# PSUM tiles taken from hand-kept lists, and a new table for the order of all steps, in a chunked RWKV-7 kernel with a low-rank mixer behind it

## The chip, the cores and the metric

The kernel runs on one core of one Trainium2 chip. The metric is device time in microseconds (us) of one execution; the time before is the median of seven.

## What is computed

The reference has two blocks. The first is a recurrence over 768 time steps, for 4 batches of 8 heads with a 40 x 40 state each:

```python
for t in range(S):
    y[:, :, t] = einsum('bhd,bhde->bhe', rt, state)
    Sa = einsum('bhde,bhe->bhd', state, at)
    state_decay = state * wt[:, :, None, :] - einsum('bhd,bhe->bhde', Sa, bt)
    state = state_decay + einsum('bhd,bhe->bhde', vt, kt)
```

Its output, put into the form (4, 768, 320), is `x` of the second block:

```python
h = x.transpose(0, 2, 1) @ U @ V          # low-rank mixing along time, rank 32
u = x + h.transpose(0, 2, 1)
ch = maximum(u @ w_ch1, 0.0) @ w_ch2      # 320 -> 1280 -> 320
return u + ch
```

All is float32.

## The kernel before

**Two phases.** Phase 1 does the recurrence in chunks of 64 time steps. A unit is one chunk of one pair of batches: 2 pairs x 12 chunks = 24 units, numbered 0 to 23, where units 0 to 11 belong to the first pair. Phase 2 is the mixer's two large matmuls (`up_proj`, lines 259 to 265, and `down_proj`, line 273), for six blocks of four chunks.

**The steps of phase 1.** Each unit is worked off by Python generators, and each `next()` of one issues a small step:

- `f` (`prep_f`, 8 steps a unit): clip the decay w (f.1); transpose w and a on TensorE into the PSUM tiles `pw` and `pa`, and scan `pw` on VectorE, line 456 (f.2); multiply `pa` into `fa` (f.3); transpose the scan into `pq`, copied out by ScalarE (f.4); reciprocal on VectorE (f.5); scale b on GpSimd (f.6); transpose it into `pb` (f.7); scores into `pf`, written to DRAM by four DMAs (f.8).
- `l` (`substitute`, 17 steps for a group of units): the triangular inverse, 30 rounds of a multiply and an add, on VectorE for unit 0 (`l0`) and on GpSimd for the groups 1 to 3, 4 to 7, and so on (`l1` to `l6`). A `g` step before it gathers the scores by DMA, and a `t` step after it fetches the result (`td`) for one unit.
- `s` (`prep_s`, 9 steps): transposes of v, r, k (`pv`, `pr`, `pk`), scores (`pe`) and the assembly of the inverse (`pg2`, `px2`).
- `c` (`carry`, 11 steps): the recurrence itself, with the PSUM tiles `ph`, `ps`, `pg`, `pX`, `pn`, `pd`, `pS`.
- `q` and `p` are squares for a range check on ScalarE; capital letters load one input of one unit; `w` loads and narrows the float64 weights of the mixer, seven small steps for each piece; `m` runs the mixer's first block ahead (`hut`, `mix`, `turn`).

Nearly every step that uses TensorE issues one block of matmuls there: 4 of 128 x 128, or 32 small ones. I call that a group. Phase 1 has some 553 of them.

**What sets the order.** A string `ORDER` (line 735) lists 1312 steps, and a loop issues them one by one; a suffix says on which queue a DMA is issued (`s` or none: SyncE, `a`: ScalarE, `x`: half on each). The engines' queues are in order, so the table decides what stands before what on every engine.

**Where PSUM tiles come from.** [...]`one(name)` takes a tile of one bank from a pool of two, `two(name)` one of two banks from a pool of three. Which of the pool's places a tile gets is chosen by the framework when it places the program's tiles:

```python
        def one(name):
            return ps.tile([128, 512], F32, name=name, tag="one", bufs=2)

            pw = one("pw")
            up(wc, pw)
            pa = one("pa")
            up(u.nat["A"], pa)
            nc.vector.tensor_copy(seg[:, :, 0:1], heads(pw[:])[:, :, 0:1])
```

The first matmul into a tile waits for whatever read the place's last tile.

Of the kernel before, what the change touches and what calls it, by code (L numbers as in the profile page):

```python
# [37 lines left out]
def kernel(  # L38
# [138 lines left out]
    def hut(pr, bank, new):  # L177

        ps_ = [bank(f"ph{x}") for x in range(2)]
        for c in range(NCH):  # L180
            for x in range(2):
                nc.tensor.matmul(out=ps_[x][32 * (c % 4):32 * (c % 4) + 32, 0:DM], lhsT=U_[half(x), c, :],
                                 rhs=XTM[half(x), pr * NCH + c, :], start=c < 4, stop=c >= NCH - 4,
                                 skip_group_check=True)
        hs = [new() for _ in range(2)]
        nc.vector.tensor_copy(hs[0][:, 0:DM], ps_[0][:, 0:DM])
        nc.scalar.activation(out=hs[1][:, 0:DM], in_=ps_[1][:, 0:DM], func=ACTF.Copy)
        ts = []
        for x in range(2):
            p = bank("pq")  # L190
            nc.tensor.matmul(out=p[0:RANK, 0:DM], lhsT=IB[:], rhs=hs[x][:, 0:DM], start=True, stop=True)
            ts.append(new()[0:RANK, 0:DM])
            nc.vector.tensor_copy(ts[x], p[0:RANK, 0:DM])
        return ts

    def mix(g, ts, bank):

        pr, th = g // NT, g % NT
        for c in range(th * GC, (th + 1) * GC):
# [5 lines left out]
            nc.vector.tensor_tensor(out=x, in0=p[:, 0:DM], in1=x, op=ALU.add)  # L205
            yield

    def turn(g, bank, new, uf):

        for i in range(3):  # L210
# [10 lines left out]
            if i == 1:  # L221
                nc.scalar.activation(out=t, in_=p[:], func=ACTF.Copy)
            else:
                nc.vector.tensor_copy(t, p[:])
            uf.append(t)
            yield

    def ahead(bank):

        first["ts"] = ts = hut(0, bank, dead)  # L230
        yield
        for g in range(NT):
            for i, _ in enumerate(mix(g, ts, bank)):
# [3 lines left out]
        yield from turn(0, bank, lambda i: dead(), first["uf"])  # L237
# [3 lines left out]
    def part_2(ex, again):  # L241
# [3 lines left out]
        def bank(name):  # L245
            return mps.tile([128, 512], F32, name=name, tag="pm", bufs=2)

# [33 lines left out]
        if again:  # L281
            ts, uf = hut(0, bank, new), []
            for g in range(NT):
                for _ in mix(g, ts, bank):
                    pass
            for _ in turn(0, bank, piece, uf):
                pass
        for g in range(NG):
            hid = mb.tile([128, NJ, 2 * GN], F32, name="hid")
            up_proj(hid, uf, (0, 2))  # L290
            if g + 1 == NT:
                ts = hut(1, bank, new)
            up_proj(hid, uf, (4,))
            if g + 1 < NG and g + 1 >= NT:
                for _ in mix(g + 1, ts, bank):
                    pass
            up_proj(hid, uf, (6, 8))
            if g + 1 < NG:
                uf = []
                for _ in turn(g + 1, bank, piece, uf):  # L300
# [7 lines left out]
    with ExitStack() as p1:  # L308
# [77 lines left out]
        def one(name):  # L386
            return ps.tile([128, 512], F32, name=name, tag="one", bufs=2)

        def two(name):
            return ps.tile([128, 2, 512], F32, name=name, tag="two", bufs=3)  # L390
# [48 lines left out]
        def prep_f(u):  # L439
# [17 lines left out]
                                         initial=1.0, op0=ALU.mult, op1=ALU.add)  # L457
            yield
# [3 lines left out]
            nc.vector.tensor_copy(u.fa[:, :, 0:1], heads(pa[:])[:, :, 0:1])  # L462
            u.fa = u.fa[:].rearrange("p (i x) t -> p i (x t)", x=2)
# [6 lines left out]
            for s, t in enumerate((u.x[:, 0], qo[:])):  # L470
                nc.scalar.activation(out=t, in_=p[:].rearrange("p (i s e) -> p s i e", s=2, e=DP)[:, s, :, 0:D],
                                     func=ACTF.Identity, scale=at0[:, 0:1], bias=at0[:, 1:2])
            across(nc.scalar, u, qo)
# [14 lines left out]
            nc.scalar.activation(out=fb[:].rearrange("p i t -> p (i t)"), in_=p[:], func=ACTF.Copy)  # L488
            yield
# [6 lines left out]
            for q, t in enumerate((fl, u.fh)):  # L496
# [3 lines left out]
                for x in range(2):  # L500
                    nc.sync.dma_start(out=u.fd[x, :, q].rearrange("h (s t) -> s h t", t=LB),
                                      in_=t[64 * x + 32 * q:64 * x + 32 * q + 32])
            yield
# [47 lines left out]
        def prep_s(u):  # L551
# [7 lines left out]
            nc.scalar.activation(out=fv[:].rearrange("p i t -> p (i t)"), in_=pv[:], func=ACTF.Copy)  # L559
            yield  # L560
# [3 lines left out]
            nc.scalar.activation(out=u.fr[:].rearrange("p i t -> p (i t)"), in_=pr[:], func=ACTF.Copy)  # L564
            yield
# [3 lines left out]
            nc.scalar.activation(out=fk[:].rearrange("p i t -> p (i t)"), in_=pk[:], func=ACTF.Copy)  # L569
            yield  # L570
# [16 lines left out]
            masked(u.cm[:], p[:, :, NP * DP:])  # L587
            yield
# [10 lines left out]
            for x in range(2):  # L599
                s = slice(64 * x + 32, 64 * x + 64)  # L600
                nc.scalar.activation(out=GX[s, :, 0:32],
                                     in_=pg[s, 0:NH * 32].rearrange("p (h t) -> p h t", t=32), func=ACTF.Copy)
            yield
            px = one("px2")
            for h in range(NH):
                for x in range(2):
# [4 lines left out]
                                 func=ACTF.Copy)  # L611
            yield
# [3 lines left out]
        def carry(u):  # L616
# [5 lines left out]
            pv = two("ph")  # L622
            for i, s, x in four:
                nc.tensor.matmul(out=pv[half(x ^ s), s, D * i:D * (i + 1)], lhsT=u.e[half(x), s, i, :],  # L624
                                 rhs=vt[half(x), 2 * i + s, 0:D], start=True, stop=True)
            pv = pv[:, :, 0:NP * D].rearrange("p s (i e) -> p s i e", e=D)
# [3 lines left out]
            nc.scalar.activation(out=rs if first else ve[:], in_=pv, func=ACTF.Copy, scale=-1.0)  # L630
            yield
            if not first:
                p = two("ps")
                for i, s, x in four:
# [3 lines left out]
                                        op=ALU.subtract)  # L638
            yield
# [9 lines left out]
            for i in range(NP):  # L649
                for x, s in ((0, 0), (1, 1), (0, 1), (1, 0)):  # L650
# [5 lines left out]
                                 in_=p[:, :, 0:NP * DP].rearrange("p x (i t) -> p x i t", t=DP), func=ACTF.Copy)  # L656
            yield
# [11 lines left out]
            if not last:  # L669
# [3 lines left out]
                nc.scalar.activation(out=nx[:], in_=heads(p[:])[:, :, 0:D], func=ACTF.Copy)  # L673
            yield
# [13 lines left out]
            if not last:  # L688
# [8 lines left out]
                nc.vector.tensor_tensor(out=state["K"][:, :, :, 0:D], in0=dn, in1=pe, op=ALU.mult)  # L697
            yield
# [8 lines left out]
            for s, t in enumerate((u.x[:, 0], yo[:])):  # L707
                nc.vector.scalar_tensor_tensor(out=t, in0=py[:, s], scalar=1.0, in1=u.x[:, s], op0=ALU.mult,
                                               op1=ALU.mult, accum_out=SQ[:, u.n, NCHK - 2 + s:NCHK - 1 + s])
            across(nc.sync, u, yo)  # L710
            yield
            if not last:
# [7 lines left out]
                nc.scalar.activation(out=SV[:], in_=heads(p[:])[:, :, 0:D], func=ACTF.Copy)  # L720
                yield
# [14 lines left out]
W0 W1a B1x A0 V1a f0 A1x B0x p1 f0 W2x q1 f0 A2 f0 K1x f1 q0 f0 f0 R1x f1 f1 w q0 V2 B2x W3x f1 f2 f1 f0 q1 A3x f2  # L736
f3 f0 f1 W4x f2 f2 f2 f1 K0x f3 f3 q3 f4 q2 g0x B3 f1 p2 f2 W5 f3 l0 q3 f3 g1a f2 f3 p1 l0 l0 A4 f2 q4 V0 s1 l0 s0
f3 p1 R0a f4 f3 B4x l0 f5 k g2 p0 f4 B5 f4 g3a l1 W6 l0 q4 l1 A5a f4 s0 q2 s0 s0 f4 A6 q5 l0 s1 f5 s1 l1 l0 p0 f6
R2a w f5 l0 p2 f6 l0 l0 f6 l1 B6 f5 l1 s0 K3 A7x W7x q6 l1 q6 q5 l1 l0 f4 f5 l1 f7 A8x q8 l0 f5 w l1 l0 f6 B7x f4
l0 q7 f5 l1 l1 W9 f7 l0 f6 W8x l0 f7 A9a f6 l1 p0 f5 c0 g4 f7 f7 f6 f7 t0 l1 s0 s0 f6 c0 f7 s0 g5a l1 f7 K2 w c0 w  # L740
l1 s0 f8 g6x f8 c0 l1 l1 g7 s1 f8 c0 c0 c0 t1x l2 f8 q7 A10x l2 l2 c0 s1 c0 s1 c0 B8 s1 f8 l2 s1 c0 c1 s1 f8 c1 s2
W10 q10 f10 c1 f9 l2 p2 V3x c1 s2 f8 w c1 c1 s2 q8 q9 t2 f9 c1 f9 c1 l2 c1 R3 V4 s2 f8 c1 t3 f9 s2 l2 s2 s3 l2 s3
f9 s2 s2 w c2 p3 l2 c2 l2 R4x c1 B9 p3 s2 w c2 p3 s3 A11x f10 f10 p4 c2 W12x s3 K4 W11x c2 w B10 f9 l2 c2 c2 f10
s3 c2 c2 c2 A12 f9 q9 V5 R5 s3 s3 w q10 f11 l2 c2 c3 p4 c3 s3 w s4 s4 l2 f9 l2 l2 s3 c3 q12 s4 s4 B11x l2 l2 f10
c3 K5 p5 R6x f11 t4x W13 f11 w c3 c3 s4 t5 s4 f10 B12x c3 f10 c3 q11 f11 c3 c3 s5 c4 A13 f11 p5 s4 s4 c3 f10 f12
c4 p5 s4 f11 s5 c4 f11 w s5 w g8 f13 V6 c4 f11 s5 g10 c4 s5 c4 f12 s5 p6 c4 s5 w q12 g11 p4 f12 g9a K6x l3 f12 c4
t6 c4 c5 w l3 s5 c4 c5 V7x c4 q13 s6 s6 s5 f12 f13 A14 p6 q11 c5 f13 W15 p6 c5 w f12 A15x s6 w s6 c5 w K7x W14 l3
s6 R7 l3 f14 c5 l3 s6 c5 t7 c5 l3 l3 q14 p7 R8 B13 s6 f13 s6 c5 f13 c5 c6 c5 c6 q15 l3 w s6 p7 f13 f14 V8 f14 q13
c6 l3 p7 f15 c6 s7 w B14 c6 w c6 l3 f12 f14 f12 f14 s7 c6 s7 c6 f13 s7 w s7 l3 c6 f15 W16 f15 w l3 l3 q14 K9 V9a
l3 R9x s7 w A17 f13 s7 w K8 s7 f15 c6 l3 c7 c6 w W17x c7 l3 s7 s8 s8 g12x c7 c7 l3 f15 c7 A16a c7 g13x s8 c7 c7  # L750
B15 p8 f14 t8 s8 f14 f15 s8 p9 s8 f14 c7 p9 f15 c7 f16 s8 s8 f15 w g14 c7 c8 q15 s8 q17 s9 g15x B16 W18 p8 c8 l4
c8 s9 s9 V10 c8 f16 R10 f17 t9 l4 p8 c8 q16 K10 l4 c8 c8 f16 w c8 s9 A18 W19x f16 s9 c8 s9 s9 l4 R11 c8 p9 c8 K11
s10 s10 l4 l4 f16 s9 c9 t10 V11 f16 s10 p10 s9 w w l4 l4 c9 f17 c9 f17 c9 s10 s10 B17 A19 q16 w c9 f17 f17 c9 p11
f17 l4 l4 p11 s10 f19 f16 c9 c9 c9 s10 V12 p11 c9 B18 p10 s11 s10 s11 l4 c10 l4 l4 q19 c9 s11 c10 l4 s10 t11 R12
c10 R13 W21 f18 p10 f17 K12 f18 q18 c10 f18 f16 c10 A20 q17 s11 c10 l4 w s11 f19 W20x p12 K13x q18 l4 c10 f19 s11
p12 f18 s11 c10 c10 l4 c10 B19 s11 f18 t12 f20 c10 f19 c11 c11 g16a s11 c11 s12 s12 s12 c11 V13 s12 f19 f18 f17 w
s12 s12 V14x s12 f21 A21x f18 c11 s12 c12 f18 s12 w c12 f20 c11 c12 c11 c11 p12 K14a t13 f19 c11 c12 f19 c11 q20
s13 f20 c12 f19 s13 s13 w g18 s13 R14 p13 c12 c12 g19a s13 W22a s13 f21 c12 g17x c12 l5 f21 w w l5 s13 V15 c12 q21
B20 q19 s13 p14 w w f20 c12 w c13 l5 s14 s13 c13 p13 B21 l5 f20 f20 A23 p14 R15 s14 s14 c13 c13 t14 p13 f21 A22 l5
c13 K15 w W23 l5 l5 s14 c13 t15x c13 p15 w f22 s14 s14 q20 c13 f20 s14 c14 c13 f21 w q21 c14 l5 s14 c13 p15 c13  # L760
# [164 lines left out]
```

## Time and profile before

| what | value |
|---|---|
| median of 7 runs | 839.5 us (835.47 to 852.36) |
| the profiled execution | 846.28 us, its span 844.5 us |
| granted TensorE clock, mean | 0.889 |
| busy: TensorE matmul / VectorE / GpSimd / ScalarE | 708.4 / 412.3 / 298.7 / 254.2 us |

In the names of the profile, PE is TensorE's matmuls, PEld its weight loads, DVE VectorE, ACT ScalarE, POOL GpSimd, SP SyncE; a q behind a name is that engine's DMA queue. Busy time says nothing of what waits for what; for that there are the waits (who sat idle until what ended), the timeline (instructions in order of time) and the windows (busy time in stretches of the span). Phase 2 begins at about 541 us.

### The profile page before, as it was taken

The page shows a single profiled execution, that of the slowest core. Times are in us where ns is not written, and L with a number is a line of the kernel's source. Part 1 is how long each engine was busy: PE and PEld are TensorE (multiplying, and loading weights), DVE is VectorE, ACT ScalarE, POOL GpSimd, SP SyncE. Part 2 cuts the span into 40 slices and gives each one's busy share as a digit, 9 for nine tenths or more (in the row PEclk, how much of TensorE's full clock was granted, in tenths as well). Part 3 has the DMA queues.
Part 4 walks back from the last instruction along what each step waited for, and adds up shares of the span by engine and source line. Part 5 has one row for each costly group of instructions (what it writes and reads, how often), then busy time and mean ns, then how long its engine had stood idle before and what let it go on. Part 6 is the DMA issues. An engine that isn't in the chain of part 4 may idle for free.

```text
span 844.5 us, 30102 instructions
## 1 busy us (share of the span) xinstructions
PE 708.4 (84%) x13146; PEld 505.0 (60%) x13146; DVE 412.3 (49%) x854; ACT 254.2 (30%) x662; POOL 298.7 (35%) x541
## 2 busy tenths in 40 slices
PE   4543778798788878887886888899999999999996
PEld 2433667687676767776774776446473553735554
DVE  7899657577836664796675677210112112121110
ACT  2432345454553643554343444010101001000000
POOL 3457478227717640782698445000000000000000
PEclk9755599888987896799797899799999999999998
DMA  7553445655545464646453432001010010100101
GB/s 126 100 106 54 86 76 94 113 93 85 88 105 89 82 120 72 111 77 132 86 105 101 98 91 62 5 1 32 0 24 9 4 28 0 24 9 8 24 8 26
DMA packets 241386, 53.87 MB, mean 64 GB/s; under 512 B 233728, under 2 KB 236832, under 8 KB 241248
## 3 DMA queue, kind: packets, MB, share of 16 engines
q1 hardware_dynamic: 182864, 42.14, 25.9%
q10 hardware_dynamic: 58384, 9.74, 6.8%
q8 instruction: 105, 1.72, 0.9%
q14 instruction: 33, 0.27, 0.1%
HBM read 37.68 MB, written 10.22 MB: 57 GB/s over the span
## 4 chain that ended last, share of the span: by engine, by line
PE 65%; DVE 10%; DMA 7%; issue 7%; POOL 4%; ACT 3%; SPq 2%; ACTq 1%; DVEq 0%; POOLq 0%
PE p L273 15%; PE p L259 13%; PE p L262 4%; PE px L608 3%; PE pS L717 3%; PE pe L430 2%; PE pg L597 2%; PE pd L681 1%; PE ph L624 1%; PE pg L704 1%; PE pq L424 1%; PE ps L635 1%; PE pX L652 1%; PE pv L202 1%; PE pg L663 1%
## 5 line engine op out<-in xcount | busy, mean ns | idle before, releaser
L273 PE MATMUL p<-ip,hid 128*128 128x320 f32 x384 | 107.3, 432 | 0.0
L531 POOL TENSOR_TENSOR ln<-ln,tmp 128x30 f32<-128x30 f32 (+19 forms) x180 | 97.9, 544 | 14.1
L529 POOL TENSOR_TENSOR tmp<-ln 128x30 f32<-128x30 f32 (+19 forms) x180 | 93.8, 521 | 12.1
L259 PE MATMUL p<-uf,W 128*128 128x512 f32 x200 | 95.4, 621 | 0.0
L264 ACT ACTIVATE hid<-p 128x512 f32<-128x512 f32 x30 | 17.9, 597 | 256.9 <-PE p L262 256.9
L273 PEld LDWEIGHTS p<-ip,hid 128*128 128x128 f32 x384 | 73.0, 190 | 30.4
L265 DVE TENSOR_SCALAR hid<-p 128x512 f32<-128x512 f32 x30 | 20.7, 692 | 127.0 <-PE p L262 127.0
L259 PEld LDWEIGHTS p<-uf,W 128*128 128x128 f32 x200 | 37.5, 195 | 53.0 <-issue 52.2
L276 DVE TENSOR_TENSOR o<-p,XTM 128x320 f32<-128x320 f32 x24 | 11.8, 492 | 117.3 <-PE p L273 117.3
L478 DVE RECIPROCAL ip<-ip 128x320 f32<-128x320 f32 x24 | 51.7, 2153 | 0.8
L554 POOL TENSOR_TENSOR nKT<-nK,ip 128x320 f32<-128x320 f32 x24 | 21.9, 914 | 56.4 <-PE pg L704 32.6
L483 POOL TENSOR_TENSOR nBT<-nB,ip 128x320 f32<-128x320 f32 x24 | 20.7, 864 | 58.1 <-DMA nB<-in_b_dram 18.6
L717 PE MATMUL pS<-ID,SK 64*64 64x64 f32 x704 | 30.0, 238 | 7.9 <-issue 6.0
L608 PE MATMUL px<-t,GX 32*64 32x32 f32 x768 | 32.3, 235 | 2.6 <-issue 2.1
L717 PEld LDWEIGHTS pS<-ID,SK 64*64 64x64 f32 x704 | 26.4, 150 | 9.5 <-issue 6.8
L608 PEld LDWEIGHTS px<-t,GX 32*64 32x64 f32 x768 | 29.2, 152 | 4.8 <-issue 2.7
L419 PE MATMUL pw<-ID,nWC 128*128 128x128 f32 x96 | 21.7, 367 | 11.0 <-DVE nWC L444 10.8
L424 PE MATMUL pq<-ID,PF 128*128 128x128 f32 x96 | 19.9, 343 | 13.1 <-DVE PF L456 10.0
L456 DVE TENSOR_TENSOR_SCAN PF<-pw,seg 128x512 f32<-128x512 f32 x24 | 29.4, 1225 | 2.6 <-DVE pw L455 0.5
L419 PE MATMUL pa<-ID,nA 128*128 128x128 f32 x96 | 20.5, 353 | 11.8 <-issue 9.6
L273 PE MATMUL p<-fa,hid 128*128 128x320 f32 x96 | 30.4, 439 | 0.0
L262 PE MATMUL p<-uf,W 64*128 64x512 f32 x100 | 28.2, 641 | 0.0
(171 smaller groups left out, 1415.0 us busy)
## 6 DMA issues: line engine op xcount, KB each, us to landing
raw<-in_moe_w_ch_dram SPq DMA_DIRECT2D x18, 320.0 KB, 3.3
out_dram<-o SPq DMA_DIRECT2D x48, 80.0 KB, 2.0
nB<-in_b_dram SPq DMA_DIRECT2D x39, 80.0 KB, 3.4
nV<-in_v_dram SPq DMA_DIRECT2D x38, 80.0 KB, 2.8
nK<-in_k_dram SPq DMA_DIRECT2D x36, 80.0 KB, 3.8
nW<-in_w_dram SPq DMA_DIRECT2D x34, 80.0 KB, 3.2
nA<-in_a_dram SPq DMA_DIRECT2D x34, 80.0 KB, 3.0
td<-ln SPq DMA_DIRECT2D x5, 512.0 KB, 3.0
```

Of the source, the lines that this page charges most:

```text
L259: nc.tensor.matmul(out=ps_[x][:], lhsT=W1[i][:, (j + x) * 128:(j + x + 1) * 128], rhs=uf[i], start=(i == 0), stop=False)
L262: nc.tensor.matmul(out=ps_[x][:], lhsT=W1[2][half(x), (j + x) * 128:(j + x + 1) * 128], rhs=uf[2][half(x)], start=False, stop=True)
L273: nc.tensor.matmul(out=p[:, 0:DM], lhsT=hid[:, f, 2 * j * L:2 * (j + 1) * L], rhs=W2[f], start=(f == 0), stop=(f == NJ - 1))
L419: nc.tensor.transpose(out=p[:, 128 * i:128 * (i + 1)], in_=t[:, 2 * i:2 * i + 2, :].rearrange("p h e -> p (h e)"), identity=ID[:])
L424: nc.tensor.transpose(out=p[:, 128 * i:128 * (i + 1)], in_=t(i), identity=ID[:])
L456: nc.vector.tensor_tensor_scan(out=pf[:, 1:], data0=pw[:], data1=seg[:].rearrange("p h t -> p (h t)"), initial=1.0, op0=ALU.mult, op1=ALU.add)
L478: nc.vector.reciprocal(out=u.ip[:], in_=u.ip[:])
L529: eng.tensor_tensor(out=x, in0=ln[:, 0:j, j:j + 1].to_broadcast([m, j, n]), in1=ln[:, j:j + 1, j + 1:].to_broadcast([m, j, n]), op=ALU.mult)
L531: eng.tensor_tensor(out=ln[:, 0:j, j + 1:], in0=ln[:, 0:j, j + 1:], in1=x, op=ALU.add)
L554: nc.gpsimd.tensor_tensor(out=kt[:, :, 0:D], in0=u.nat["K"][:], in1=u.ip[:], op=ALU.mult)
L608: nc.tensor.matmul(out=px[half(x), 32 * h:32 * h + 32], lhsT=GX[s, h, :], rhs=u.t2[s, h, :], start=True, stop=True)
L717: nc.tensor.matmul(out=p[half(s), 64 * (2 * i + x):64 * (2 * i + x + 1)], lhsT=state["K"][half(s), i, x, :], rhs=ID[half(s), half(s)], sta ...
```

## The change

The pools `one` and `two` become objects that hold their tiles for the whole of phase 1 and hand out the one that was given back first, in the order in which the Python code issues its steps. A call of `back` is put behind the last reader of each tile, also in the mixer's steps that run ahead; phase 2 keeps its own pool and passes a `back` that does nothing. The steps, their instructions and their number stay the same.

```diff
-        def one(name):
-            return ps.tile([128, 512], F32, name=name, tag="one", bufs=2)
-
-        def two(name):
-            return ps.tile([128, 2, 512], F32, name=name, tag="two", bufs=3)
+        class Banks:
+            def __init__(self, name, n, shape):
+                self.free = [ps.tile(shape, F32, name=f"{name}{i}") for i in range(n)]
+            def __call__(self, name):
+                return self.free.pop(0)
+            def back(self, *tiles):
+                self.free.extend(tiles)
+        one = Banks("one", 2, [128, 512])
+        two = Banks("two", 3, [128, 2, 512])
...
             nc.vector.tensor_tensor_scan(out=pf[:, 1:], data0=pw[:], data1=seg[:].rearrange("p h t -> p (h t)"),
                                          initial=1.0, op0=ALU.mult, op1=ALU.add)
+            one.back(pw)
             yield
...
             nc.vector.tensor_copy(u.fa[:, :, 0:1], heads(pa[:])[:, :, 0:1])
+            one.back(pa)
```

The table `ORDER` is new from its first line to its last; it has the same 1312 steps, and other queues for some of the loads. The stretch before the first step of the recurrence (`c0`), and the one around the first `m`:

```diff
-l0 q7 f5 l1 l1 W9 f7 l0 f6 W8x l0 f7 A9a f6 l1 p0 f5 c0 g4 f7 f7 f6 f7 t0 l1 s0 s0 f6 c0 f7 s0 g5a l1 f7 K2 w c0 w
...
+f3 g2a l0 g3x q4 p1 f5 k R0 l0 q2 V2a W6x l0 l1 q4 q5 s0 f4 s0 f4 f5 f6 p0 l1 R2x s0 l1 l0 l1 A6 q3 A7 f5 l0 f4 s0
+f4 f5 q7 l1 B5 f6 p1 f5 l0 l1 w q6 W7 l1 q5 p2 l1 p2 f6 l1 f4 s1 l0 f7 B7 A8x l0 l0 s1 l0 l0 l0 B6x c0 f5 l0 q7 W9
+W8x f5 g4x f6 f7 t0 f6 w p0 K2a l1 f6 l1 f7 f7 f6 f6 s1 f7 f8 f7 c0 c0 l1 s0 s0 f7 l1 s0 f7 g5a s0 p1 c0 w q6 l1
...
-w w s19 c18 s19 w l6 w R21a p19 K21a w w l6 w l6 l6 c19 c19 w w m w s20 w p21 w p20 w w c19 s20 c19 t20 s20 c19
...
+s19 w c18 w t19 w l6 w c18 s19 c18 V21a l6 w l6 p18 R21a R20a p18 s19 w K20a w V20a w p21 s19 w w w p20 l6 w p19 m
```

## The prediction

> **What bounds the kernel now.** I read the page first, then the windows, then the waits, then the timeline at the two longest TensorE waits that no data explains.
>
> The page's busy rows and 40 slices of 21.1 us each:
>
> ```profile
> PE 708.4 (84%) x13146; PEld 505.0 (60%) x13146; DVE 412.3 (49%) x854; ACT 254.2 (30%) x662; POOL 298.7 (35%) x541
> ...
> PE   4543778798788878887886888899999999999996
> ...
> DVE  7899657577836664796675677210112112121110
> ...
> PEclk9755599888987896799797899799999999999998
> ```
>
> Three stages can be seen. In slices 1 to 5 VectorE is full and TensorE half idle at a half clock; in slices 6 to 25 TensorE is at seven to eight tenths; from slice 26 (541 us) it is at nine: phase 2, some 303 us, which the change does not touch. So 541 us can move.
>
> The windows say how each stage is limited (columns: stretch, length, then busy us of PE, PEld, DVE, ACT, POOL with counts, granted clock, DMA share, GB/s):
>
> ```profile
> 80.00:90.00 10.00, 3.40 (x71) 3.02 (x72) 9.36 (x18) 0.89 (x4) 5.65 (x10) 0.50 0.36 63
> 90.00:100.00 10.00, 6.88 (x139) 5.89 (x137) 5.89 (x11) 4.67 (x12) 7.27 (x17) 0.67 0.46 86
> 100.00:110.00 10.00, 9.67 (x220) 8.09 (x220) 3.73 (x8) 2.88 (x6) 2.88 (x8) 0.59 0.51 116
> ...
> 300.00:350.00 50.00, 41.43 (x1137) 36.44 (x1140) 26.43 (x60) 20.71 (x54) 14.89 (x34) 0.73 0.54 98
> 350.00:400.00 50.00, 39.64 (x1432) 33.95 (x1427) 41.17 (x80) 25.80 (x67) 32.58 (x57) 0.99 0.53 102
> ```
>
> At 80 to 90 us VectorE is full; at 90 to 110 it does 9.6 of 20 us while TensorE catches up. From about 100 us TensorE is the bound: its gaps between 100 and 541 us add up to 37 us, those before 100 us to 43 (the timeline's gaps over 0.3 us).
>
> The waits of TensorE and VectorE in phase 1 (total, times, longest):
>
> ```profile
> DVE tt L574 <- DMA nT<-td: 24.7, 7, 5.3
> ...
> PE pw L419 <- DVE nWC L444: 10.8, 4, 7.6
> ...
> PE pa L419 <- issue: 9.6, 2, 7.8
> ...
> PE pb L419 <- POOL nBT L483: 6.7, 4, 4.0
> ...
> PE pq L191 <- DVE fa L186: 6.2, 1, 6.2
> ...
> PE pg L597 <- DVE tt L574: 5.4, 3, 2.7
> ```
>
> The third row is odd: `pa` needs only a loaded input. The timeline at the longer of its two waits, then at the other, and a group at full clock for size:
>
> ```profile
> 77.78 1.06 PE L419 MATMUL pw<-ID,nWC 128*128 128x128 f32 x4
> ...
> 85.28 1.23 DVE L456 TENSOR_TENSOR_SCAN PF<-pw,seg 128x512 f32<-128x512 f32 x1
> ...
> 86.61 1.09 PE L419 MATMUL pa<-ID,nA 128*128 128x128 f32 x4 [7.76 <-issue]
> ...
> 323.53 1.22 DVE L456 TENSOR_TENSOR_SCAN PF<-pw,seg 128x512 f32<-128x512 f32 x1
> ...
> 324.86 1.09 PE L419 MATMUL pa<-ID,nA 128*128 128x128 f32 x4 [1.85 <-issue]
> ...
> 330.97 0.66 PE L419 MATMUL pv<-ID,nV 128*128 128x128 f32 x4
> ```
>
> Both times `pa` starts 0.1 us after the scan of its own unit's `pw` ends. In the compiled program of the kernel before, which shows each tile's bank and each semaphore wait, these two `pa` (units 7 and 16) lie in the bank of their own `pw`, so TensorE stands until VectorE has scanned it. The code issues `pa` before the scan; the pool still chose that place, though another tile's reader had been issued earlier.
>
> **The change, part by part.**
>
> *Placement.* Comparing that program's banks with the rule "first given back in the order of issue" on the old table, 24 of 444 tiles have another predecessor: the two `pa`, the tiles that swap with them, three other swaps in the one-bank pool, and seven swaps of `pg` with `pX`. The swaps are worth nothing: `pX` waits 0.8 us in all. The first matmul into a pool tile also waits for TensorE itself (154 times in that program), which a kept tile would not need; these semaphore instructions take 0.05 us ahead in the weight queue, so 0 to 2 us, taken as 0. What counts is 7.76 + 1.85 = 9.6 us of TensorE standing still. The 1.85 at 323 us lies where TensorE is the bound: -1.9. The 7.76 is bounded by 0 (VectorE was 94% busy meanwhile) and 7.76; VectorE's 10.4 us of idle in the 20 us after it says that TensorE's lag came back, so I take all: -7.8.
>
> *The start of the new table.* Its own PSUM waits: unit 5's `pa` is taken at f5.2 and held to f5.3, and between them `pv`, `pq` and `pr` follow each other in the one bank left, each behind the last one's reader: a scan (0.07 + 0.17 + 1.23), a copy (0.60), two half copies (0.97), 3.0 us together. Unit 7's `pq` follows `pa` directly and waits for its scan, 1.5 us. So +4.5, and the start gives -3.3 net. As a check I summed work by mean durations up to c1's first step: 66 TensorE groups and 96 us of VectorE in the old table, 67 and 94 in the new. No more than 2 to 4 us is in that.
>
> *DMA waits in the steady stage.* In TensorE groups (480 from c1 at 113.9 us to c23 at 520.3 us: 0.85 us each) I counted how far a transfer's issue lies ahead of its use. Writing `td` took 5.7 us in the chain of waits and fetching it 3.4, together 11 groups. From the last `l` step to the first unit's `tt` the old table leaves 4, 6, 5, 7, 13.6, 9, 13 groups, 24 short; the new 8, 5.6, 15, 11, 7, 14.6, 12, which is 12 short, but three later fetches are only 1 to 2 groups ahead, 8 more. 20 for 24, of the 10.0 us that `pg` of line 597 waits (5.4 and 4.6 more put down to issue): -1.5. Loads of w: twice 0 groups and once 1 in the old table, none under 2 beyond unit 3 in the new; of 10.8 us 7.6 is the first unit's and stays: -2 of the other 3.2. Loads of b get longer leads (shortest 2, 3, 4 against 2, 6, 9): -2 of 6.7. Loads of k get shorter ones (2, 3, 6 against 5, 5.6, 6): +1.5, GpSimd being late for `pk`.
>
> *Queues.* DMAs issued on ScalarE go from 99 to 90 (each about 0.65 us), on SyncE from 309 to 318. ScalarE is half busy: 0. SyncE's transfers move later by 6 us spread over 540: 0, and at most +2 where one queues behind a blocked write.
>
> *The mixer's start.* The 6.2 us of `pq` of line 191: VectorE stood behind GpSimd, which had three `l6` steps ahead of the narrowing it waited for. In the new table TensorE is there 8.6 groups (7.3 us) earlier and GpSimd has three `l6` steps and a weight piece (8 us by their rows) less to do: -1, bounds -6 and +3.
>
> *Nearer neighbours.* `pq` directly behind its scan's `pw`, 4 times for 2; one is counted above: +1.5. `pf` directly behind `pb`, 3 for 2: +0.8.
>
> Sum: -1.9 - 3.3 - 1.5 - 2 - 2 + 1.5 - 1 + 2.3 = -7.9.
>
> *The clock.* The 50-us windows from 100 to 541 give about 116 us at the half clock, where a group takes 1.09 us for 0.66: 116 x 0.39 = 45 us lost, more than the 37 us of gaps. The Trainium skill ("TensorE: Matmul & The Clock Gate", "What's actually happening") says that the clock halves after at least one idle window of about 3.4 us. By that rule only the 6.2-us gap at 450 us costs clock here, and shorter waits saved bring nothing: -7.9. The rows disagree: at 300 to 350 us the clock is 0.73 and no gap there exceeds 2.2 us. In proportion (45 us for 37 us of gaps) the 5 us of gaps saved after 100 us would bring 6 more: -14. I take one shortened stretch of about 5 us, 5 x 0.39 = -2, and keep 0 and -6 for the range.
>
> -9.9 in all, on the profiled execution's 846.3: 836.4. That execution is 6.8 us above the median of the runs shown; as the waits that go are set by order, not by that excess, I take them whole from the median: 829.6, rounded to 830.
>
> **The rivals.** About 0.5%, 4.2 us, is what a measurement of this kernel can tell from no change.
>
> *The start is VectorE's.* Then neither the 7.8 nor the 4.5 counts, -7.9 + 3.3 - 2 and no clock leave about -5 to -3: 836. For it: 94% busy at 80 to 90 us. Against: the idle VectorE after it. Same side of nothing: 837, within the bound.
>
> *The one-bank chain at f5.2 (slower).* The chain's first wait is a scan, and the scan for the `pw` of 77.78 us, done at 78.8, began 6.4 us later, behind VectorE's other work. If it does so at f5.2 and again at unit 7's `pq`, 2 x 6 us more come in: TensorE stands as before, in two places, and `c0` with it. With +12 the sum is +2, and with the k loads and the mixer's start at their bad ends (+4 and more) 846. It decides from about 6 us of delay at each scan: below 4 us each the sum stays under zero. For it: only two banks, and VectorE full. Against: in the new table just two `l0` steps are issued between f5.2 and f5.3, and they stand behind the scan, not before it.
>
> *TensorE stays warm.* All of the proportional clock gain, and the mixer's start at its good end: -14 - 5 = -19, 821.
>
> *The placement does nothing* (the pool's choice comes back by other waits) is part of the first rival.
>
> **How the numbers follow.** Forecast (830, between 820 and 835): 0.48. Warm TensorE (821, down to 814): 0.16. VectorE's start (837): 0.20. One-bank chain (846): 0.16. Faster by over 0.5%: 0.48 + 0.16 = 0.64; within: 0.20; slower: 0.16. The range leaves out a few per cent below 815 and the upper half of the slower case: 815 to 846.
>
> **What would show it.** Right: no wait of `pa` on "issue" in the waits; `c0` near 82 us and `c1` near 111; TensorE's gaps from 100 us to the start of phase 2 at about 32 us for 37; waits of `tt` on `td` near 20 us; phase 2 starting near 531 and still 303 us long. Wrong: `pv` of unit 0 or `pq` of unit 7 waiting over 5 us for a scan; `nKT` waits on its load above 30 us; a granted clock in 100 to 541 us below before's 0.87; or phase 2 not of the same length.

## The result, and the profile after

| | before | after |
|---|---|---|
| median | 840.49 us (829.66 to 859.35, 63 runs) | 831.35 us (821.51 to 839.47, 26 runs) |
| the profiled execution, its span | 846.28, 844.5 us | 832.25, 830.5 us |
| granted TensorE clock, mean | 0.889 | 0.896 |

The ratio is 0.991, with a 95% interval of 0.9885 to 0.9934: faster by 0.9%; the medians lie 9 us apart. A second measurement of the same kernel among the experiments gave 0.9944 (0.99 to 0.9988). The forecast was 830. The time came out as forecast; most of the sum behind it did not.

In the changed kernel all one-bank tiles are called `one` and all two-bank tiles `two`. Old lines 419, 424, 430, 456, 191, 574 and 597 are now 435, 440, 446, 472, 192, 598 and 622. The page's rows, 40 slices of 20.8 us each:

```profile
PE 703.9 (85%) x13146; PEld 500.5 (60%) x13146; DVE 400.2 (48%) x854; ACT 253.2 (30%) x662; POOL 296.3 (36%) x541
...
PE   3645799789888789887848899899999999999996
...
DVE  6888677567657747575645757111102112021110
...
PEclk9856599989999969799877978999999999999998
```

The same three stages. Phase 2 now begins at 523.6 us (before: 537.0, and not 541, as the prediction has it) and lasts 306.9 us (before 307.5). So 13.4 us of this pair of executions are gained ahead of it. The profiled execution of before is one of its slower ones, 5.8 us above the median, and that of after is 0.9 above, so some 5 of the 13.4 us are no part of the change. The windows that answer to those of before, in the same columns:

```profile
80.00:90.00 10.00, 2.21 (x8) 1.44 (x8) 9.41 (x23) 1.38 (x5) 3.70 (x8) 0.50 0.50 91
90.00:100.00 10.00, 8.86 (x171) 7.61 (x172) 4.43 (x8) 4.87 (x13) 8.48 (x19) 0.50 0.38 65
100.00:110.00 10.00, 9.53 (x335) 8.06 (x337) 6.60 (x18) 3.99 (x13) 6.57 (x16) 0.91 0.55 120
```

At 80 to 90 us TensorE works even less than before (2.21 us for 3.40) while VectorE is as full (9.41 for 9.36). The timeline there shows what took the place of the wait of `pa`:

```profile
78.10 1.11 PE L435 MATMUL one<-ID,nA 128*128 128x128 f32 x4
...
83.68 1.23 DVE L472 TENSOR_TENSOR_SCAN PF<-one,seg 128x512 f32<-128x512 f32 x1
...
84.96 1.12 PE L440 MATMUL one<-ID,PF 128*128 128x128 f32 x4 [5.75 <-DVE PF L472]
```

`pa` of unit 7 now starts directly behind its `pw`, and then TensorE stands 5.75 us at `pq`, the next tile, for the same scan. The scan comes late because VectorE is behind: it is busy for 9.41 of the 10 us. Whether it matters which TensorE step waits for it, `hand_seq` below tells.

The waits of the changed kernel that answer to those shown of before (total, times, longest):

```profile
DVE tt L598 <- DMA nT<-td: 19.4, 10, 6.4
...
PE one L440 <- DVE PF L472: 12.7, 7, 5.7
...
PE one L192 <- DVE fa L186: 8.5, 1, 8.5
...
PE one L435 <- DVE nWC L460: 8.4, 2, 7.6
...
PE one L435 <- POOL nBT L502: 5.9, 2, 3.3
...
PE one L192 <- ACT fa L187: 5.2, 1, 5.2
...
PE one L622 <- DVE tt L598: 4.9, 3, 2.5
```

The long wait of `pa` on issue is gone. The mixer's start, line 192, has two waits, 13.7 us together, for 6.2. One window from 100 us to the start of phase 2, of before and then of after, shows both parts of the gain:

```profile
100.00:536.90 436.90, 362.90 (x11528) 309.89 (x11524) 283.08 (x611) 198.43 (x528) 245.49 (x418) 0.87 0.49 93
```

```profile
100.00:523.60 423.60, 354.88 (x11485) 302.85 (x11483) 274.61 (x612) 196.06 (x528) 243.36 (x417) 0.88 0.50 96
```

Of 13.3 us, TensorE's idle time gives 5.3 (74.0 to 68.7) and its busy time 8.0: nearly the same matmuls, run faster. This is one pair of executions; the experiments ask what makes the matmuls run faster.

### The profile page after: what moved, and what is told of

Read it like the earlier page. It is cut to its first block, busy times and chain, and to the rows that moved or that the text cites. A ratio compares the mean times of both kernels' runs of the same rounds, so it can differ in the third digit from the quotient of the medians.

```text
span 830.5 us, 30105 instructions
## 1 busy us (share of the span) xinstructions
PE 703.9 (85%) x13146; PEld 500.5 (60%) x13146; DVE 400.2 (48%) x854; ACT 253.2 (30%) x662; POOL 296.3 (36%) x541
## 4 chain that ended last, share of the span: by engine, by line
PE 58%; POOL 9%; DMA 9%; DVE 8%; issue 7%; SPq 5%; ACT 3%; ACTq 1%; POOLq 0%; DVEq 0%
PE p L280 16%; PE p L266 14%; PE one L435 4%; PE p L269 4%; POOL tmp L550 3%; POOL ln L552 3%; PE two L446 2%; PE one L634 2%; PE two L712 2%; PE one L750 2%; DMA fd<-fh 2%; SPq L521 2%; PE one L440 2%; SPq L340 2%; DMA nR<-in_r_dram 1%
## 5 line engine op out<-in xcount | busy, mean ns | idle before, releaser
L550 POOL TENSOR_TENSOR tmp<-ln 128x30 f32<-128x30 f32 (+19 forms) x180 | 93.9, 521 | 12.3
L283 DVE TENSOR_TENSOR o<-p,XTM 128x320 f32<-128x320 f32 x24 | 11.8, 492 | 117.3 <-PE p L280 117.3
L634 PE MATMUL one<-t,GX 32*64 32x32 f32 x768 | 30.8, 232 | 2.3 <-issue 1.2
L440 PE MATMUL one<-ID,PF 128*128 128x128 f32 x96 | 19.7, 340 | 14.9 <-DVE PF L472 12.6
L750 PE MATMUL one<-ID,SK 64*64 64x64 f32 x704 | 31.0, 249 | 0.8 <-issue 0.8
L634 PEld LDWEIGHTS one<-t,GX 32*64 32x64 f32 x768 | 27.9, 148 | 4.9 <-issue 1.9
L472 DVE TENSOR_TENSOR_SCAN PF<-one,seg 128x512 f32<-128x512 f32 x24 | 29.4, 1225 | 2.3
L750 PEld LDWEIGHTS one<-ID,SK 64*64 64x64 f32 x704 | 27.9, 161 | 2.0 <-issue 1.0
L435 PE MATMUL one<-ID,nR 128*128 128x128 f32 x96 | 19.2, 332 | 11.5 <-DMA nR<-in_r_dram 5.6
L544 POOL TENSOR_SCALAR_AFFINE_SELECT ln<-ln 128x1024 f32<-128x1024 f32 (+2 forms) x7 | 8.8, 1264 | 55.8 <-DMA ln<-fd 42.6
L435 PE MATMUL one<-ID,nWC 128*128 128x128 f32 x96 | 20.4, 350 | 9.5 <-DVE nWC L460 8.4
```

The lines of the kernel that those rows point to most:

```text
L435: nc.tensor.transpose(out=p[:, 128 * i:128 * (i + 1)], in_=t[:, 2 * i:2 * i + 2, :].rearrange("p h e -> p (h e)"), identity=ID[:])
L440: nc.tensor.transpose(out=p[:, 128 * i:128 * (i + 1)], in_=t(i), identity=ID[:])
L472: nc.vector.tensor_tensor_scan(out=pf[:, 1:], data0=pw[:], data1=seg[:].rearrange("p h t -> p (h t)"), initial=1.0, op0=ALU.mult, op1=ALU.add)
L550: eng.tensor_tensor(out=x, in0=ln[:, 0:j, j:j + 1].to_broadcast([m, j, n]), in1=ln[:, j:j + 1, j + 1:].to_broadcast([m, j, n]), op=ALU.mult)
L634: nc.tensor.matmul(out=px[half(x), 32 * h:32 * h + 32], lhsT=GX[s, h, :], rhs=u.t2[s, h, :], start=True, stop=True)
L750: nc.tensor.matmul(out=p[half(s), 64 * (2 * i + x):64 * (2 * i + x + 1)], lhsT=state["K"][half(s), i, x, :], rhs=ID[half(s), half(s)], sta ...
```

## The experiments

Ratios are to the kernel before, in runs on the same chip; those of one paragraph can be compared directly unless it says otherwise.

**The two halves alone.** `hand_old` is the changed kernel with the old table, `pool_new` the old kernel with the new table.

```diff
 # hand_old: the changed kernel
-ORDER = """ (new table)
+ORDER = """ (old table)
 # pool_new: the kernel before
-ORDER = """ (old table)
+ORDER = """ (new table)
```

> The kept tiles with the OLD table: the placement alone. Theory A (the gain is mostly the two waits of pa behind its own scan, 9.6 us of TensorE): 831 to 834 us against 840, no wait of pa on a scan, c1 some 5 to 8 us earlier than at 113.9 us. Theory B (the gain is the table; the long wait of 7.76 us lay beside a full VectorE and costs nothing): 837 to 840 us, only the 1.85-us wait in the steady stage is saved.

> The pools with the NEW table: the table alone. In its program one pa (unit 7) still lies in the bank of its own pw. Theory A: the table alone brings little, 836 to 840 us, with a long wait of pa on its scan at about 80 us. Theory B: nearly all of the gain, 830 to 833 us, though that wait is there.

`hand_old`: 837.65 us, ratio 0.9879 (0.9815 to 0.9943). `pool_new`: 849.48 us, 1.0053 (1.0019 to 1.0087). The kept tiles bring the whole gain, and the table by itself loses 4.5 us. With kept tiles the table changes nothing that can be seen (0.9879 without it, 0.991 and 0.9944 with it, in other sets of runs). My working gave the table a gain of its own.

**The stall at the mixer's start.** `m_early` puts the first `m` of the changed table 25 steps earlier (what was expected says 27, a miscount). Run with the two above:

```diff
-... s19 w c18 w t19 w l6 w c18 s19 c18 V21a ... l6 w p19 m
+... s19 w c18 w t19 w l6 w c18 m s19 c18 V21a ... l6 w p19
```

> The changed kernel with the first m step (hut) moved 27 steps ahead, in front of step s19.5 (the transpose of tt, which waits for a DMA). In the changed kernel TensorE stands 8.5 and 5.2 us in hut, because its two copies are queued on VectorE behind tt and a narrowing that waits for GpSimd, and on ScalarE behind loads. Theory A (the waits are in the queues ahead of the copies, and TensorE is the bound there): both waits under 2 us in all and 820 to 825 us against 831. Theory B (GpSimd, behind with the last substitution, sets the pace of this stage whatever TensorE does): the waits go elsewhere, 829 to 832 us.

It gave 833.17 us, ratio 0.9779 (0.9703 to 0.9855; six runs). The waits of its TensorE from 400 to 450 us:

```profile
PE one L634 <- ACT GX L626: 8.9, 1, 8.9
...
PE one L192 <- DVE fa L186: 0.7, 1, 0.7
```

The stall has moved from line 192 to `px2`, line 634. The ratio is lower than the changed kernel's in another set of runs, but a change of place alone does not show why; see `early_16`.

**Which pool.** `hand_two` keeps the two-bank tiles and lets the framework's pool place the one-bank tiles; `hand_one` is the reverse. `after_again` is the changed kernel.

```diff
 # hand_two
-one = Banks("one", 2, [128, 512])
+one = Pooled("one", 2, [128, 512])      # ps.tile(..., tag="one", bufs=2); back() does nothing
 # hand_one
-two = Banks("two", 3, [128, 2, 512])
+two = Pooled("two", 3, [128, 2, 512])
```

> The changed kernel itself, on the same chip as the three below, so that they can be set against it. Every theory: 0.991 of the kernel before, within half a per cent.

> New table; the two-bank tiles kept by hand, the one-bank tiles from their pool as before (one pa again in the bank of its pw; some 150 first matmuls wait for TensorE's own semaphore). Theory A (what the pools cost lies in the one-bank pool): like the new table with both pools, 1.003 to 1.007 of before. Theory C (it lies in the swaps of pg, ps and pX among the two-bank tiles, 14 here): 0.990 to 0.994.

> New table; the one-bank tiles kept by hand, the two-bank tiles from their pool. Theory A: 0.990 to 0.994 of before, as the changed kernel. Theory C: 1.003 to 1.007.

`after_again` 836.25 us, 0.9944 (0.99 to 0.9988). `hand_two` 848.27, 1.0026 (0.9993 to 1.0059). `hand_one` 839.98, 0.9935 (0.9891 to 0.9979). So the gain lies in the one-bank tiles: 0.8%, 7 us, with intervals that do not meet. The two-bank tiles matter nothing that can be seen.

`hand_two` has the wait of `pa` of unit 7 back (8.1 us on issue in its waits), yet the first copy of `c1` comes at 110 us in it, at 111 in the profile after and at 112 in that of `after_again`. The wait that I had put first among the gains does not move the start.

**The weights' narrowing.** In the same set of runs, `narrow16` gives VectorE six weight pieces that GpSimd narrowed, to shorten what stands ahead of the mixer's start:

```diff
-            todo = dst, raw, nc.vector if n < 10 else nc.gpsimd
+            todo = dst, raw, nc.vector if n < 16 else nc.gpsimd
```

> The changed kernel with six more pieces of the mixer's weights narrowed wholly on VectorE instead of half on GpSimd (three operations a piece: 2.6 us of GpSimd become 2.0 us of VectorE). Theory A (the 8.5 and 5.2 us of TensorE in hut hang on GpSimd, which is full from 400 to 450 us and gives the weight buffers back late): both shrink by half or more and the time is 3 to 8 us below the changed kernel. Theory B (GpSimd's last substitution sets the pace, or VectorE's added 12 us come back as waits): within 2 us of it, or slower by up to 5.

833.18 us, ratio 0.984 (0.9761 to 0.9918), which overlaps `after_again`'s interval: a gain of 1% is possible and not shown. The first stall remained (the narrowing now stands on VectorE ahead of the mixer's copy); of its waits from 400 to 450 us:

```profile
PE one L192 <- DVE fa L186: 8.9, 1, 8.9
PE two L712 <- issue: 1.3, 1, 1.3
PE one L192 <- ACT fa L187: 1.2, 1, 1.2
```

**Where the tiles lie, or how they are given out.** A kept tile and a pool tile differ in two things: the bank, and the release. A new pool tile makes its first matmul wait for everything that used the place's last tile, TensorE's own matmuls among it. In the compiled programs TensorE waits for its own semaphore 30 times in the changed kernel and 176 times in `hand_two` (the traces show 12 and 158, the same difference); all engines issue the same work in the same order in both. Only four pairs of one-bank tiles of `hand_two` have changed places with each other; the last is `pa` of unit 7 with the tile behind it. Two kernels separate the two things. `hand_seq` has kept tiles in the pool's banks; `pool_seq` has pool tiles, one pool of a single buffer per bank, in the changed kernel's banks.

```diff
 # hand_seq
-                return self.free.pop(0)
+                return self.free.pop(self.calls in (14, 18, 29))     # for the one-bank tiles
...
-            pa = one("pa")
-            up(u.nat["A"], pa)
+            pa = one("pa") if u.n != 7 else pw       # unit 7: pa is issued behind the scan
 # pool_seq
-                return self.free.pop(0)
+                k = self.free.pop(0)
+                t = ps.tile(self.shape, F32, name=name, tag=f"{self.name}{k}", bufs=1)
```

> The changed kernel's persistent tiles, but its one-bank tiles in the banks that the pool chose: one choice reversed at the pb of unit 2, at the pw of unit 5 and at the pr of unit 1, and the pa of unit 7 in its own pw's bank, issued after the scan. Every engine does the same work in the same order as in hand_two; only the releases differ. Theory A (where the tiles lie, above all the own bank of unit 7): about 848 us, ratio 1.002 like hand_two, c1 at 111. Theory B (a pool tile makes TensorE wait on its own semaphore, some 146 more waits than persistent tiles): about 836, ratio 0.994 like the changed kernel, although the pa of unit 7 waits some 8 us at 76 us.

> The mirror image: the one-bank tiles lie where the changed kernel has them, but each bank is a pool of one buffer, so every tile is a new pool tile that waits for the last release, and TensorE has 148 waits on its own semaphore more than in the changed kernel. No pa waits on issue. Theory A (where the tiles lie): about 836 us, ratio 0.994. Theory B (the pool's extra waits on TensorE): about 848, ratio 1.002, and a mean granted clock near 0.88 against 0.90.

`hand_seq` 830.25 us, 0.9888 (0.9828 to 0.9948); `pool_seq` 842.5 us, 0.9993 (0.9961 to 1.0025). It is the release and not the place. In `hand_seq` the wait I had counted as 7.76 us is there in full, 8.43 us, and the kernel is as fast as the changed one; its timeline:

```profile
76.15 1.06 PE L436 MATMUL one<-ID,nWC 128*128 128x128 f32 x4
85.64 1.12 PE L436 MATMUL one<-ID,nA 128*128 128x128 f32 x4 [8.43 <-DVE PF L474]
```

**Both small changes together.** In the same set, `early_16` is `m_early` and `narrow16` in one kernel.

> The changed kernel with the first m moved in front of the first c18-s19 steps (as m_early) and the weight pieces 10 to 15 narrowed on VectorE (as narrow16). If the two small gains are independent: narrow16 1.0 % and m_early up to 1 % below the changed kernel, ratio 0.975. If both only take away the same stall, which comes back at px2 or at the mixer's copies: ratio 0.984 to 0.99, no better than narrow16 alone.

828.94 us, ratio 0.985 (0.9781 to 0.9919), no better than `narrow16` alone and not to be told from `hand_seq` beside it. The wait at line 192 is 0.9 us, and another has come up at `pS`, line 750:

```profile
PE one L750 <- DVE SK L728: 6.4, 1, 6.4
```

So the mixer's stall is worth little: something else stands there when it goes. This kernel has the lowest median of all, but it is not shown to beat the changed one.

**Which of the waits.** The last two kernels split `pool_seq`: a bank's tile is made anew only for some names, and otherwise used on.

```diff
 # pool_seq, then:
+                t = self.now.get(k)
+                if t is None or name in ("pv", "pq", "pn", "pr", "pg2", "ph0", "ph1", "pu"):   # fresh_on
+                if t is None or name in ("pb", "pS", "pk", "pa", "pw", "px2"):                 # fresh_apart
                     t = ps.tile(self.shape, F32, name=name, tag=f"{self.name}{k}", bufs=1)
```

> As pool_seq (the changed kernel's banks, one pool of one buffer per bank), but a bank's tile is made anew only for pq, pv, pr, pg2, pn and the mixer's tiles ahead; for the others the bank's present tile is used on, as in the changed kernel. TensorE has 113 waits on its own semaphore (changed kernel 30, pool_seq 178): 93 ride on a matmul, 20 stand in an instruction of their own; its separate semaphore instructions are 240 (192, 269). Theory N (every own wait costs the same): 83 of pool_seq's 148 more waits, 56 % of a loss of 0.7 %: ratio 0.997. Theory E (only own waits that stand in an instruction of their own cost, because they hold up the loads ahead): 15 of 63 of them: ratio 0.994 to 0.995, like the changed kernel. Theory I (every added instruction costs): 48 of 77: ratio 0.9975.

> The other half of fresh_on: a bank's tile is made anew only for pw, pa, pb, pk, px2 and pS. TensorE has 98 waits on its own semaphore, 45 on a matmul and 53 in an instruction of their own; its separate semaphore instructions are 224. Theory N (every own wait): 68 of 148, ratio 0.996. Theory E (own waits in an instruction of their own): 48 of 63, ratio 0.998. Theory I (every added instruction): 32 of 77, ratio 0.996. If neither half shows a loss, the two halves need each other or pool_seq's loss is smaller than its interval says.

`fresh_on` 844.95 us, 0.9987 (0.9957 to 1.0016); `fresh_apart` 838.68 us, 0.989 (0.9858 to 0.9923). `fresh_on` lies near theories N and I; `fresh_apart` fits none of the three. As far as the intervals tell, the first set carries the whole loss and the second none, although it has three quarters of the additional waits that stand in an instruction of their own (48 of 63). So neither these instructions nor the number of own waits by itself is the cost: `hand_one` has 115 of them, 85 more than the changed kernel, at no loss either. What matters is at which tiles the release changes: `pq`, `pv`, `pr`, `pg2`, `pn` and the mixer's tiles.

**Where the time goes.** Two windows of each kernel, from the first copy of `c19` to that of `c21`, and from there to phase 2; the work in them is the same. `hand_seq` and `fresh_apart`, which keep the gain:

```profile
442.90:475.80 32.90, 28.32 (x1052) 24.65 (x1050) 22.31 (x57) 15.64 (x40) 15.34 (x18) 0.95 0.47 105
475.80:524.20 48.40, 41.02 (x1213) 31.99 (x1205) 32.58 (x84) 18.42 (x47) 20.82 (x25) 0.89 0.27 65
```

```profile
455.50:485.80 30.30, 27.73 (x1044) 24.47 (x1043) 24.06 (x58) 15.46 (x40) 16.39 (x20) 0.95 0.55 122
485.80:531.30 45.50, 39.63 (x1218) 31.53 (x1211) 30.70 (x82) 18.75 (x47) 19.99 (x24) 0.92 0.27 64
```

`pool_seq` and `fresh_on`, which lose it:

```profile
444.30:479.40 35.10, 32.93 (x1055) 28.45 (x1052) 22.75 (x58) 15.60 (x40) 15.29 (x19) 0.78 0.44 100
479.40:534.60 55.20, 48.36 (x1211) 37.84 (x1203) 32.59 (x83) 18.66 (x47) 20.76 (x25) 0.72 0.23 57
```

```profile
449.50:484.20 34.70, 32.33 (x1041) 28.54 (x1036) 22.87 (x58) 15.63 (x39) 15.69 (x19) 0.80 0.48 107
484.20:539.80 55.60, 49.78 (x1219) 38.94 (x1212) 30.87 (x83) 18.63 (x47) 20.09 (x25) 0.71 0.22 52
```

The stretch takes 81.3 and 75.8 us in the first two, 90.3 and 90.3 in the other two. TensorE's idle time does not explain it (12.0 and 8.4 us for 9.0 and 8.2); its busy time does (69.3 and 67.4 for 81.3 and 82.1), at a clock of 0.89 to 0.95 for 0.71 to 0.80. Most other kernels with the new table fall on the same sides: 81.8 us in the profile after and 82.1 in `after_again` (clock 0.80 to 0.93 in both), 89.7 in `hand_two` and 85.4 in `pool_new`. `hand_one`, which keeps the gain, lies between with 86.0, in an execution 4.7 us above its median.

These are single executions, and this stretch is not always the place. `hand_two` is 10 us later than `after_again` at `c19` already, and `fresh_apart` 6 us later there than `fresh_on`. In the kernel before, whose table has other steps around it, the stretch takes 82.9 us although its tiles come from pools; of the 13.4 us against the profile after, 12.3 lie between 100 us and `c19`, 11.8 of them busy time.

The timeline shows one place. In `hand_seq`, then in `pool_seq`, the same three groups:

```profile
486.32 0.63 PE L657 MATMUL two<-nV,e 64*64 64x40 f32 x32
486.88 0.66 PE L441 MATMUL one<-ID,xf 128*128 128x128 f32 x4
...
488.90 0.69 PE L628 MATMUL one<-tt,fh 32*32 32x32 f32 x32
```

```profile
484.97 0.50 PE L461 MATMUL two<-fr,fv 64*64 64x64 f32 x18 [1.41 <-issue]
...
488.97 1.04 PE L666 MATMUL two<-nV,e 64*64 64x40 f32 x32
489.94 1.11 PE L455 MATMUL pn<-ID,xf 128*128 128x128 f32 x4
...
492.86 1.06 PE L637 MATMUL pg<-tt,fh 32*32 32x32 f32 x32
```

No group waits there in either; each takes 1.04 to 1.11 us for 0.63 to 0.69. In the 8 us ahead of them `pool_seq` has one wait of 1.41 us and one of 0.34, `hand_seq` one of 0.80, and one of 1.42 just ahead of that.

The record of the clock says what stands between. It changes in steps of 3.4 us. Two such stretches of `pool_seq`, then of `hand_seq`:

```profile
483.70:487.10 3.40, 2.13 (x89) 1.80 (x90) 1.61 (x3) 1.26 (x5) 1.73 (x3) 1.00 0.29 90
487.10:511.00 23.90, 23.90 (x454) 18.09 (x450) 12.11 (x30) 6.07 (x14) 7.65 (x9) 0.50 0.24 56
```

```profile
480.60:497.60 17.00, 15.05 (x508) 11.59 (x508) 11.04 (x25) 7.12 (x19) 8.09 (x10) 1.00 0.30 69
497.60:504.50 6.90, 6.90 (x114) 5.31 (x112) 3.15 (x8) 2.16 (x4) 2.37 (x4) 0.51 0.18 50
```

In `pool_seq` the step from 483.7 us, which holds the 1.41-us wait, has 2.13 us of matmuls; the clock then halves and stays at half for 23.9 us, in all of which TensorE is busy. What keeps it there is in the traces too: how much of the array the matmuls of a step use. Give each matmul a weight, the rows of the array that it uses times the columns that it uses times the columns of data streamed through, with 1 for 128 x 128 x 128. Then a group of four transposes weighs 4, and the 32 small matmuls of `px2` together weigh 1. The seven half-clock steps of `pool_seq` weigh 9.7, 7.6, 5.1, 6.7, 4.5, 9.3 and 14.0, and after the last the clock is full. In the 14 traces, from 100 to 530 us, each of the 966 steps that weigh over 12 is followed by a step at full clock, and of the 241 that weigh under 7 only 11 are. One limit at 9.5 tells the next step's clock in 91% of all 1762 steps; the best limit on busy time does so in 83%. This is a pattern found in the traces afterwards: no kernel here was written to try it.

Over all runs of a set the mean granted clock points the same way: 0.9021 and 0.8823 in `after_again` and `hand_two`, 0.8987 and 0.887 in `hand_seq` and `pool_seq`, 0.8899 and 0.8853 in `fresh_apart` and `fresh_on`. In 840 us, 0.02 of clock is 34 us at the half clock, and at 0.39 us lost per us there (a group takes 1.09 us for 0.66) 13 us. By this estimate the three pairs come to 13, 8 and 3 us. That is not the whole account: `hand_old` has the same mean clock as the kernel before in its set (0.8985 and 0.8986) and is 1.2% faster.

What is shown is that the way of release at these tiles costs 7 to 9 us with the new table (0.8%, 1.05% and 0.97% in three pairs), and in the profiles that the last 85 us of phase 1 then run slower without more idle time, at the half clock. Why the pool's release leads to more time at the half clock is not shown. Kept tiles also change the waits between ScalarE and VectorE (there are more of them, not fewer: 233 in the trace after, 160 in that of `hand_two`), and no kernel here changes TensorE's own waits alone; that, and the mixer's tiles alone, was not tried.

## Why the prediction held, and where it did not

The forecast of 830 and the range hold. Point by point:

- **The two `pa`.** The compiled program puts the second one in unit 20, not 16 as the prediction says. Unit 7's wait was taken whole, -7.8; it is worth about 0 (`hand_seq` has it and is as fast; a loss of 7.8 us would lie outside its interval). I argued from VectorE's idle time after it that TensorE's lag came back; the rival "the start is VectorE's" was right about this part (its own sum, -7.9 + 3.3 - 2, gives -6.6 and not -5 to -3). Unit 20's -1.9 was not tried alone.
- **The start's own waits, +4.5.** `pq` of unit 7 waited 5.75 us, not 1.5, and by my own mark, over 5 us, a sign of the rival with the one-bank chain. It cost no time for the same reason: VectorE had the work to do. The first copy of `c0` came at 73 us (forecast 82), that of `c1` at 111, as forecast.
- **TensorE's own waits, taken as 0.** This is the step that failed. I counted 154 of them and priced them by their 0.05 us in the weight queue. The way of release that they belong to is worth 7 to 9 us, nearly the whole gain, and not by the time that the waits take. Whether these waits are what costs is open: 85 of them at the two-bank tiles (`hand_one`) and 68 at half of the one-bank tiles (`fresh_apart`) cost nothing that can be seen.
- **The table's DMA waits.** `tt` waits 19.4 us for 24.7 (forecast about 20); `pw` waits 8.4 for 10.8 (-2.4, forecast -2); `pb` 5.9 for 6.7 (-0.8, forecast -2). GpSimd's `nKT` waits 0.7 us for its load, for 23.7 before: the loads of k became better, where the sum has +1.5. The first two sizes were right, but `pool_new` shows that such terms do not add up to a gain: the table alone loses 0.5%. A wait shortened by 2 us in such a list is not 2 us of time.
- **The mixer's start, -1 with bounds of -6 and +3.** It became +7.5 (13.7 for 6.2), outside the bounds. Being earlier at the place, TensorE waited longer for the narrowing and then for ScalarE's copy, which I had not looked at. With the first of these waits moved away, another stands at `px2` or `pS`.
- **The clock, -2.** In the profiles TensorE's idle time from 100 us to phase 2 fell by 5.3 us, near the 5 I expected, but the busy time fell by 8.0. The 37 us of gaps that I started from is a wrong reading: the gaps over 0.3 us there come to 69 (and 51, not 43, ahead of 100 us), so the rule of 45 us lost for 37 of gaps had no ground. Read by the Trainium skill ("TensorE: Matmul & The Clock Gate", "What's actually happening"), which lets the clock halve after an idle window of about 3.4 us, these kernels should not differ at their end. They do: in the stretch shown no wait of `pool_seq`'s TensorE exceeds 2.0 us, and its clock is 0.72 to 0.78; the measurement decides. A rule in proportion to idle time would not have found it either, since the idle time is about the same (9.0 us for 12.0). What the clock goes with in these traces is the weight of the matmuls in a step, as above.

Right total, wrong split: the gains I gave to the two `pa` and to the table stand for one that I had set to nothing. That the total came out at 830 is luck.

## What to carry to other kernels

Before a visible wait is priced, ask whether its releaser would be any earlier without it: here the same late scan stopped TensorE one tile further on, and putting the 8-us wait back cost nothing. Try holding PSUM tiles for a whole phase where a pool's tiles follow each other closely: here it gave 0.8 to 1% at the one-bank tiles and nothing at the two-bank ones. Compare a version with the pool's places and kept tiles before crediting the places. When equal work takes different time, compare TensorE's busy time with its idle time over the same steps: here slow without idle was the half clock, which no list of waits shows. Then look at how much of the array the matmuls of that stretch use.

## What the hardware showed that I had not expected

TensorE can stay at the half clock while it is never idle. A window of the changed kernel:

```profile
490.00:500.00 10.00, 10.00 (x202) 7.66 (x200) 6.21 (x17) 1.21 (x3) 3.30 (x4) 0.54 0.33 83
```

It is busy for all 10 us at a clock of 0.54, and the longest wait of its TensorE from 476 us on to there is 0.45 us. The matmuls there are small: three steps of 3.4 us from 487.4 us on weigh 6.3, 5.9 and 4.8, under the limit found above. Two programs with the same instructions in the same order on every engine, apart from semaphore waits and PSUM banks, ran at different mean clocks: 0.9021 in `after_again` and 0.8823 in `hand_two`, over 22 runs each. The record of the clock agrees with the durations here: in `hand_seq` it is half from 497.6 to 504.5 us, and groups of four 128 x 128 matmuls take 1.11 us at 500.0 and 0.66 at 505.6.
